# Where setup work and two convolution taps stand in the order of a fused convolution and feed-forward kernel

## The chip, the cores and the metric

The kernel runs on one core of one Trainium2 chip. The metric is the device time of one execution in microseconds (us); the time before the change is 2389.32 us, the median of three runs (2388.79 to 2389.75).

The core has a matrix engine (TensorE, PE in the profile), three engines for elementwise work (VectorE or DVE, ScalarE or ACT, GpSimd or POOL), and a queue (SyncE, SP) that issues the transfers used here. Each engine takes its instructions in the order in which the program gives them; engines wait for each other through semaphores.

## The reference

A depthwise causal convolution over seven tokens, whose taps come from a softmax and are shared within a head, is followed by a feed-forward block with the activation h * sigmoid(1.702 h). Everything is in 32-bit floats.

```python
# x: (8, 4096, 192), weight: (8, 7); w_in: (192, 2048), w_out: (2048, 192)
w = softmax(weight, axis=-1)
x_pad = concat([zeros((B, 6, D)), x], axis=1)
x_unf = x_pad[:, arange(S)[:, None] + arange(7)[None, :], :].reshape(B, S, 7, H, group)
a = einsum('hk,bskhg->bshg', w, x_unf).reshape(B * S, D)      # 32768 tokens x 192
h = a @ w_in
g = h * (1.0 / (1.0 + exp(-1.702 * h)))
out = g @ w_out
```

## The kernel before

The tokens are handled in 32 steps ("big" in the code) of 1024 tokens. A step has a part `hidden` (convolved tokens times w_in, then the activation) and a part `output` (times w_out). Both replace block products by fewer products of sums of blocks; T1 and T2 are such sums of activations, made by DVE. `hidden` runs twice per step, for `v` 0 and 1. What DVE has to prepare for a later step (turning x with three transposes, then 7 convolution taps for each of three groups of channels, then block sums) is kept in a list, `todo`. At fixed places the code calls `work(us)`, which hands DVE as many items from the list as the given time allows, by the cost noted with each item.

Before step 1 the weights are made ready. They arrive as 64-bit words and are turned into 32-bit floats in eight pieces, four of w_in (pieces 0 to 3) and four of w_out (4 to 7): a DVE part (`split_piece`), an ACT part (`split_rest`), then `join_piece` and `round_piece` on DVE. Step 0 is computed by plain products meanwhile (`plain`), since the sums of weights that the other steps use (`sums_w_in`) are not made yet. Blank lines are left out below.

```python
# load_x(big): eight transfers of x into xin, of which there is one buffer; xs below has its place too
# ... (cut)
# conv_t: 13 blocks of T columns per buffer, 3 buffers; TERMS lists the 21 products
at = [(osbs, 0), (flat_room, 3 * PIECE), (places, 0), (b22, 0)]
assert 5 * PIECE + R <= 10 * TOK and 2 * PIECE <= min((NA - 4 * NC) * UW, 4 * TOK)
raw = [t[:, i : i + 2 * PIECE].bitcast(U32) for t, i in at]
# ... (cut) scratch() cuts a place into three parts m, l, e
sets = [
    scratch(own(1).rearrange("p b t -> p (b t)")),
    scratch(flat_room),
    None,
    scratch(w_out_s[:, S1 : S4 + 1, :, :].rearrange("p i f d -> p (i f d)")),
]
SET = (0, 1, 2, 0, 1, 3, 1, 3)
# ... (cut)
def words(i):
    w = raw[i % NW].rearrange("p (n w) -> p n w", w=2)
    return (w[:, :, 0], w[:, :, 1]) + tuple(sets[SET[i]])
CLAMP = (0, 3, 4)
def split_piece(i):
    lo, hi, m, l, e = words(i)
    ef = e.bitcast(F32)
    vec.tensor_scalar(m, hi, 0xFFFFF, 1 << 20, op0=ALU.bitwise_and, op1=ALU.bitwise_or)
    vec.tensor_scalar(e, hi, 20, 0x7FF, op0=ALU.logical_shift_right, op1=ALU.bitwise_and)
    if i in CLAMP:
        vec.tensor_scalar(
            ef, e, float(LOW + 255), float(LOW), op0=ALU.min, op1=ALU.max
        )
def split_rest(i):
    lo, hi, m, l, e = words(i)
    ef = e.bitcast(F32)
    act.activation(l.bitcast(F32), lo, AF.Copy, scale=2.0**-32)
    if i in CLAMP:
        act.activation(e, ef, AF.Identity, bias=bias[:, 3:4], scale=2.0**23)
    else:
        act.activation(ef, e, AF.Relu, bias=bias[:, 0:1])
        act.activation(ef, ef, AF.Relu, bias=bias[:, 1:2], scale=-1.0)
        act.activation(e, ef, AF.Identity, bias=bias[:, 2:3], scale=-(2.0**23))
def join_piece(i):
    lo, hi, m, l, e = words(i)
    vec.tensor_tensor(out=m.bitcast(F32), in0=l.bitcast(F32), in1=m, op=ALU.add)
def round_piece(i, dsts):
    lo, hi, m, l, e = words(i)
    vec.scalar_tensor_tensor(
        out=e, in0=hi, scalar=1 << 31, in1=e, op0=ALU.bitwise_and, op1=ALU.bitwise_or
    )
    for view, dst in dsts:
        vec.scalar_tensor_tensor(
            out=dst,
            in0=view(m.bitcast(F32)),
            scalar=2.0**-20,
            in1=view(e.bitcast(F32)),
            op0=ALU.mult,
            op1=ALU.mult,
        )
# ... (cut) round_w_in(i): round_piece into w_in_s
def load_w_out(i):
    nc.sync.dma_start(
        out=raw[i].rearrange("p (c d) -> p c d", c=CW),
        in_=w_out_v[:, i * CW : (i + 1) * CW, :],
    )
def round_w_out(i):
    join_piece(NW + i)
    k, j = divmod(i * CW, NK)
    round_piece(
        NW + i,
        [
            (
                lambda v, m=m: v.rearrange("p (b m d) -> p b m d", m=2, d=Q)[:, :, m, :],
                w_out_s[:, 2 * m + k, j : j + CW, :].rearrange("p j (c d) -> p (j c) d", d=Q),
            )
            for m in range(2)
        ],
    )
# ... (cut)
def prepare(big):
    for c in range(NC):
        yield "", 0.7, lambda c=c: transpose_x(big, c)
    if big + 1 < N_BIG:
        yield "", 0.0, lambda: load_x(big + 1)
    v1 = place(big, V1)
    for c in (0, 2):
        for k in range(K):
            yield "", 0.76 if k else 0.48, lambda c=c, k=k: conv(big, c, k)
    yield "", 0.38, lambda: sums_c(big, 0)
    yield f"first {big}", 0.0, lambda: cross_when(True, big, v1, v1 + 1)
    for k in range(K):
        yield "", 0.76 if k else 0.48, lambda k=k: conv(big, 1, k)
    yield "", 0.0, lambda: cross_when(False, big, 0, C31)
    for i in range(1, len(SUMS_C)):
        yield "", 0.38, lambda i=i: sums_c(big, i)
    rest = (C31, V8) if big % 2 else (C31 + 1, NB)
    yield f"all {big}", 0.0, lambda: cross_when(False, big, *rest)
def product1(slot, a, b, big, v, first=False):
    pair = conv_t[:, big % 2 : big % 2 + 2, place(big, b), :]
    for h in range(2):
        src = pair[halves[h], :, :] if h == big % 2 else pair[halves[h], ::-1, :]
        nc.tensor.matmul(
            slot[:, h, :],
            w_in_s[halves[h], a, v * P : (v + 1) * P],
            src,
            start=first,
            stop=True,
            skip_group_check=True,
        )
def terms(big, v, slot, *ts, first=False):
    for t in ts:
        product1(slot, *TERMS[t], big, v, first)
        first = False
# ... (cut)
def sum_1(*a):
    sum_g(T1, B12, B11, *a)
def sum_2(*a):
    sum_g(T2, B22, T1, *a)
def plain(u, m, n, v, slot, ks=range(NC)):
    for k in ks:
        product1(slot, NC * (2 * u + m) + k, 2 * k + n, 0, v, k == ks[0])
def hidden(big, v, x, z, y, sums, work, fetch, last=lambda: None):
    def pe(slot, *ts, first=False):
        terms(big, v, slot, *ts, first=first)
    if v:
        pe(z, 7, first=True)
        give(True, big)
    pe(sums, 12)
    act.copy(k15, sums)
    pe(x, 5, 17)
    gelu(B11, 0, v, x)
    if not v:
        pe(z, 7, first=True)
    pe(sums, 0)
    act.copy(k16, sums)
    last()
    work(3.2 if v else 1.5)
    pe(y, 6, 14, first=True)
    vec.tensor_sub(x, z, k15)
    work(2.6)
    pe(sums, 13)
    act.copy(k19, sums)
    pe(x, 2)
    act.copy(k18, x)
    pe(z, 11)
    pe(sums, 20, 10)
    vec.tensor_sub(k15, y, k19)
    # ... (cut) more terms, copies and gelus, with work(1.1), work(2.3), work(1.2), work(0.7)
def output(big, ra, rb, work, cols=ALL, between=None, end=None):
    W = cols.stop - cols.start
    small = W < TOK
    js = slice(cols.start // Q, cols.stop // Q)
    v1, v2 = u1[:, 0:W], u2[:, 0:W]
    v3, v4 = p3[:, js, :], p4[:, js, :]
    some = dict(cols=cols, small=small)
    p1, p3c = product2(ra, 0, (A11, B11), (S4, B22, 0), **some)
    act.copy(v1, p1)
    act.copy(chunk(v3, 0), blocks(p3c))
    if not small:
        work(3.0)
        sum_1(0)
        sum_2(0)
    sum_1(1, cols, small)
    sum_2(1, cols, small)
    work(0.7)
    # ... (cut) the products p2, p6, p5 and p7, their additions, turns and stores, with work(0.7), work(4.0)
def work(us):
    while todo and todo[0][1] <= us + 0.2:
        us -= todo[0][1]
        todo.pop(0)[2]()
def need(label):
    while any(item[0] == label for item in todo):
        todo.pop(0)[2]()
# ... (cut)
def first_step(fetch):

    # ... (cut) the convolution of step 0, most of it on TensorE
    xs = xin_pool.tile([P, 2, NJ, XW], F32, name="xin")
    sets[2] = scratch(xs.rearrange("p n j d -> p (n j d)"))
    split_piece(0)
    split_rest(0)
    take_conv(2, 0)
    join_piece(0)
    round_w_in(0)
    load_w_out(0)
    split_piece(1)
    take_conv(1, 1)
    split_rest(1)
    for k in range(K):
        conv(0, 2, k, second)
    copy_over(C32)
    plain(0, 0, 0, 0, slots[0])
    plain(0, 0, 0, 1, sums)
    gelu(B11, 0, 0, slots[0])
    gelu(B11, 0, 1, sums)
    for k in range(K):
        conv(0, 0, k, second)
    copy_over(C12)
    plain(0, 0, 1, 0, slots[1], (1, 2, 0))
    plain(0, 0, 1, 1, slots[2])
    join_piece(1)
    round_w_in(1)
    load_w_out(1)
    split_piece(2)
    gelu(B12, 0, 0, slots[1])
    split_rest(2)
    gelu(B12, 0, 1, slots[2])
    def rounds(now, then):
        if now < NW:
            join_piece(now)
            round_w_in(now)
            load_w_out(now)
        else:
            round_w_out(now - NW)
        if then < 2 * NW:
            split_piece(then)
            split_rest(then)
    def last_piece():
        rounds(7, 8)
        sums_w_out()
        todo.extend(("", 0.42, lambda i=i: sums_w_in(i)) for i in range(len(SUMS_W)))
        todo.append(("sums", 0.0, lambda: None))
    def piece_3():
        rounds(3, 4)
        load_x(1)
        todo.extend(prepare(1))
    between = [
        lambda: rounds(2, 3), piece_3, None, lambda: rounds(4, 5), None, lambda: rounds(5, 6),
        None, lambda: rounds(6, 7), None, last_piece, None, None,
    ]
    free = [slots[0], sums, slots[1], slots[2]]
    for u, m in ((0, 1), (1, 0), (1, 1)):
        for n in range(2):
            for v in range(2):
                slot = free.pop(0)
                free.append(slot)
                plain(u, m, n, v, slot)
                gelu(2 * m + n, u, v, slot)
                (between.pop(0) or (lambda: work(1.3)))()
    give(False, 0)
    # ... (cut) step 0's first half of output by plain products, then need("all 1"),
    # prepare(2), output(0, ..., slice(T, TOK), fetch) and need("sums")
```

Of the kernel before, what the change touches and what calls it, by code (L numbers as in the profile page):

```python
# [15 lines left out]
def kernel(  # L16
# [38 lines left out]
    NC = D // R  # L55
# [150 lines left out]
    NW = 4  # L206
# [4 lines left out]
    places = w_in_s[:, 4 * NC : NA, :].rearrange("p a f -> p (a f)")  # L211
    b12, b22 = (g[:, b, 1, :, :, :].rearrange("p v h t -> p (v h t)") for b in (B12, B22))
    at = [(osbs, 0), (flat_room, 3 * PIECE), (places, 0), (b22, 0)]
    assert 5 * PIECE + R <= 10 * TOK and 2 * PIECE <= min((NA - 4 * NC) * UW, 4 * TOK)
    raw = [t[:, i : i + 2 * PIECE].bitcast(U32) for t, i in at]
    diag = b12[:, 0 : 2 * K * R].rearrange("p (c k q) -> p c k q", c=2, k=K)
# [55 lines left out]
        nc.gpsimd.memset(bias[:, i : i + 1], b)  # L272

    def words(i):
        w = raw[i % NW].rearrange("p (n w) -> p n w", w=2)
        return (w[:, :, 0], w[:, :, 1]) + tuple(sets[SET[i]])


# [65 lines left out]

    def load_w_out(i):
        nc.sync.dma_start(
            out=raw[i].rearrange("p (c d) -> p c d", c=CW),
            in_=w_out_v[:, i * CW : (i + 1) * CW, :],
        )

# [157 lines left out]
    def sum_1(*a):  # L508
        sum_g(T1, B12, B11, *a)
# [7 lines left out]
    def sum_4(*a):  # L517
        sum_g(T4, T2, B21, *a)

    def plain(u, m, n, v, slot, ks=range(NC)):  # L520

        for k in ks:
            product1(slot, NC * (2 * u + m) + k, 2 * k + n, 0, v, k == ks[0])

    def hidden(big, v, x, z, y, sums, work, fetch, last=lambda: None):

# [15 lines that stand above are left out]
        pe(sums, 0)  # L542
        act.copy(k16, sums)
        last()
        work(3.2 if v else 1.5)
        pe(y, 6, 14, first=True)
        vec.tensor_sub(x, z, k15)  # L547
        work(2.6)
# [7 lines that stand above are left out]
        gelu(B12, 0, v, sums)  # L556
        pe(x, 4)
        act.copy(k20, x)
        vec.tensor_sub(k19, z, k19)  # L559
        work(1.1)  # L560
        gelu(B22, 1, v, k19)
        gelu(B22, 0, v, k15)
        pe(y, 8)
        pe(sums, 1, 9, first=True)
        pe(y, 15)
        work(2.3)
        vec.tensor_add(k20, k20, sums)  # L567
        vec.tensor_sub(k16, y, k16)
        gelu(B11, 1, v, k20)
        pe(x, 18)  # L570
        gelu(B21, 1, v, x)
        fetch()
        if not v:

            act.copy(y, z)
        gelu(B21, 0, v, k16)
        work(1.2)
        pe(sums, 3, 19)
        work(0.7)
        vec.tensor_add(k18, k18, sums)  # L580
        return lambda: gelu(B12, 1, v, k18)
# [58 lines left out]
# [14 lines that stand above are left out]
            work(3.0)  # L654
            sum_1(0)
            sum_2(0)
        sum_1(1, cols, small)
        sum_2(1, cols, small)
        work(0.7)
        p2, p3c = product2(rb, 0, (A12, B21), (S4, B22, 1), **some)  # L660
        act.copy(chunk(v3, 1), blocks(p3c))  # L661
        vec.tensor_add(v2, v1, p2)
        turn(0, 0, blocks(v2), js)
        sum_4(0, cols, small)
        sum_4(1, cols, small)
        p6, p3c = product2(ra, 1, (S2, T2), (S4, B22, 2), **some)
        act.copy(chunk(v3, 2), blocks(p3c))
        vec.tensor_add(v2, v1, p6)
        sum_3(0, cols, False)
        sum_3(1, cols, False)  # L670
        work(0.7)
        if between:
            between()
        p5, p4c = product2(rb, 1, (S1, T1), (A22, T4, 0), **some)
        q = quarters(rb, 0, A22, T4, 2, **some)
        act.copy(chunk(v4, 0), blocks(p4c))  # L676
        vec.tensor_add(v1, v2, p5)  # L677
        act.copy(chunk(v4, 2), blocks(q[2]))
        vec.tensor_add(v3, blocks(v1), v3)  # L679
        for l in (0, 1, 3):  # L680
            vec.tensor_add(chunk(v4, 2), chunk(v4, 2), blocks(q[l]))  # L681
        turn(0, 1, v3, js)
        work(1.5 if small else 4.0)
        parts = [(cols, ra)]
        if end is not None:
            parts = [(slice(0, T), ra), (slice(T, TOK), end)]
        done = [product2(r, 0, (S3, T3), (A22, T4, 1), cols=c, small=small) for c, r in parts]
        for (c, _), (p7, p4c) in zip(parts, done):
            k = slice(c.start - cols.start, c.stop - cols.start)
            i = slice(c.start // Q, c.stop // Q)  # L690
            act.copy(chunk(p4, 1)[:, i, :], blocks(p4c))
            vec.tensor_add(v1[:, k], v1[:, k], p7)  # L692
            vec.tensor_add(v2[:, k], v2[:, k], p7)  # L693
            turn(1, 1, blocks(v1[:, k]), i)
            vec.tensor_sub(blocks(v2[:, k]), blocks(v2[:, k]), p4[:, i, :])  # L695
            turn(1, 0, blocks(v2[:, k]), i)
            store(big, i)
# [3 lines left out]
# [4 lines that stand above are left out]
# [27 lines left out]
    def first_step(fetch):  # L732
# [28 lines left out]
        for k in range(K):  # L761
            conv(0, 2, k, second)
        copy_over(C32)
        plain(0, 0, 0, 0, slots[0])
        plain(0, 0, 0, 1, sums)
        gelu(B11, 0, 0, slots[0])
# [1 line left out]
        for k in range(K):  # L768
            conv(0, 0, k, second)
        copy_over(C12)  # L770
        plain(0, 0, 1, 0, slots[1], (1, 2, 0))
        plain(0, 0, 1, 1, slots[2])
        join_piece(1)
        round_w_in(1)
        load_w_out(1)
        split_piece(2)
        gelu(B12, 0, 0, slots[1])
        split_rest(2)
        gelu(B12, 0, 1, slots[2])

        def rounds(now, then):
            if now < NW:
                join_piece(now)
                round_w_in(now)
                load_w_out(now)
            else:
                round_w_out(now - NW)
            if then < 2 * NW:
                split_piece(then)
                split_rest(then)  # L790

        def last_piece():
            rounds(7, 8)
            sums_w_out()
            todo.extend(("", 0.42, lambda i=i: sums_w_in(i)) for i in range(len(SUMS_W)))
            todo.append(("sums", 0.0, lambda: None))

        def piece_3():
            rounds(3, 4)
            load_x(1)  # L800
            todo.extend(prepare(1))

        between = [
            lambda: rounds(2, 3), piece_3, None, lambda: rounds(4, 5), None, lambda: rounds(5, 6),
            None, lambda: rounds(6, 7), None, last_piece, None, None,
        ]
        free = [slots[0], sums, slots[1], slots[2]]
        for u, m in ((0, 1), (1, 0), (1, 1)):
# [3 lines that stand above are left out]
                    free.append(slot)  # L812
                    plain(u, m, n, v, slot)
                    gelu(2 * m + n, u, v, slot)
                    (between.pop(0) or (lambda: work(1.3)))()
        give(False, 0)


# [4 lines left out]
            sum_1(u, slice(T, TOK), True)  # L823
            sum_2(u, slice(T, TOK), True)
        js = slice(0, T // Q)
        work(6.5)
        for k in range(2):
            for i, (m, n) in enumerate(quarter):
                c, c22c = product2(
                    slots[i % 2],  # L830
                    i // 2,
                    ((A11, A12, A21, A22)[2 * m + k], (B11, B12, B21, B22)[2 * k + n]),
                    ((A21, A22)[k], (B12, B22)[k], i),
                    first=(k == 0),
                    cols=cols,
                )
                if k == 1:
                    if i == 0:
                        vec.tensor_sub(*(w_out_s[:, j, :, :] for j in (S3, A11, A21)))
                    turn(m, n, blocks(c), js)  # L840
                    act.copy(chunk(c22, i), c22c)
                    work(2.5)
        turn(1, 1, blocks(c22), js)
        store(0, js)
        need("all 1")
# [59 lines left out]
```

## Time and profile before

| | busy us | share of the span (2387.3 us) | instructions |
|---|---|---|---|
| PE, matmuls | 2357.3 | 99% | 16794 |
| PEld, weight loads (beside the matmuls) | 889.5 | 37% | 16794 |
| DVE | 1946.2 | 82% | 2182 |
| ACT | 1023.3 | 43% | 1160 |
| POOL | 8.3 | 0% | 29 |

The transfers moved 133.66 MB, at a mean of 56 GB/s. Busy time counts an instruction from its start to its end as the trace has it; the ends of matmuls are modelled, and neighbours overlap a little. A group of instructions is written as line, engine, operation, tile written <- tiles read. "PE slot L486 <- DVE slot L547" in the list of waits means that a matmul of line 486 that writes the tile `slot` stood until DVE's instruction of line 547 on `slot` had ended. The lines that matter here: 286, 287 and 289 are `split_piece`; 297 to 304 `split_rest`; 308 `join_piece`; 313 and 317 `round_piece`; 332 to 340 sums of blocks (of weights in `w_in_s`, of tokens in `conv_t`); 346 loads a piece of w_out; 100 loads x; 408 turns x; 423 and 425 are convolution taps; 486 is `product1`, 503 the activation, 506 the sums such as T1 and T2, 547 the subtraction in `hidden` shown above, 590 a product of `output`, 625 a transpose of results.

### The profile page before, as it was taken

What the parts mean: (1) busy time and instruction counts of PE and PEld (TensorE: products, weight loads), DVE (VectorE), ACT (ScalarE), POOL (GpSimd) and SP (SyncE); (2) the same over time, 40 slices, a digit from 0 to 9 for tenths busy, and PEclk for the clock granted to TensorE, in tenths of its full rate; (3) what the DMA queues carried; (4) which work ended last, traced back from release to release, by engine and by line L of the source; (5) the groups of instructions that cost most, each with busy time, mean ns of one, the idle gap of its engine ahead of it and who ended that gap; (6) DMA issues with size and microseconds to landing.
All of it is one profiled execution on the core that took longest, in us unless ns stands there. A gap on an engine that the chain in (4) does not pass through costs nothing.

```text
span 2387.3 us, 39095 instructions
## 1 busy us (share of the span) xinstructions
PE 2357.3 (99%) x16794; PEld 889.5 (37%) x16794; DVE 1946.2 (82%) x2182; ACT 1023.3 (43%) x1160; POOL 8.3 (0%) x29
## 2 busy tenths in 40 slices
PE   8999999999999999999999999999999999999998
PEld 4533333333333333333333333333333333333333
DVE  6888887888887888878888778888788887788866
ACT  5345433454333554334543345543345433455433
POOL 1000000000000000000000000000000000000000
PEclk9999999999999999999999999999999999999999
DMA  7242133231232321323312323213233123231010
GB/s 164 59 79 55 28 65 61 59 67 32 52 65 54 68 54 29 65 58 62 67 30 54 65 55 68 52 32 64 58 64 68 27 56 66 54 67 43 16 41 14
DMA packets 197724, 133.66 MB, mean 56 GB/s; under 512 B 108848, under 2 KB 188080, under 8 KB 193584
## 3 DMA queue, kind: packets, MB, share of 16 engines
q1 hardware_dynamic: 196448, 130.92, 27.2%
q8 instruction: 131, 2.15, 0.4%
q10 hardware_dynamic: 1104, 0.26, 0.1%
q14 instruction: 41, 0.34, 0.0%
HBM read 53.15 MB, written 25.17 MB: 33 GB/s over the span
## 4 chain that ended last, share of the span: by engine, by line
PE 79%; DVE 17%; issue 1%; ACT 1%; DMA 1%; SPq 0%; ACTq 0%; DVEq 0%
PE slot L590 28%; PE slot L486 28%; PE sums L486 12%; PE sums L590 9%; DVE conv_t L425 5%; DVE osbs L681 3%; DVE osbs L625 3%; PE slot L607 2%; DVE slot L547 2%; DVE room L677 1%; DVE room L692 1%; DVE osbs L679 1%; DVE room L693 1%; ACT osbs L676 1%; DVE room L695 1%
## 5 line engine op out<-in xcount | busy, mean ns | idle before, releaser
L486 PE MATMUL slot<-conv_t,w_in_s 64*128 64x512 f32 x3740 | 863.3, 595 | 21.8 <-ACT g L503 8.5
L590 PE MATMUL slot<-g,w_out_s 128*32 128x512 f32 (+1 forms) x6800 | 788.6, 571 | 0.0
L486 PEld LDWEIGHTS slot<-conv_t,w_in_s 64*128 64x128 f32 x3740 | 358.1, 188 | 482.9 <-issue 381.2
L425 DVE SCALAR_TENSOR_TENSOR conv_t<-xt,cw,conv_t 128x512 f32<-128x512 f32 (+1 forms) x576 | 423.9, 736 | 11.9
L590 PEld LDWEIGHTS slot<-g,w_out_s 128*32 128x32 f32 x6800 | 240.3, 110 | 457.1 <-issue 438.3
L486 PE MATMUL sums<-conv_t,w_in_s 64*128 64x512 f32 x1660 | 405.1, 591 | 0.0
L503 ACT ACTIVATE g<-room 128x1024 f32<-128x1024 f32 x310 | 321.1, 1058 | 108.4 <-DVE room L567 68.6
L590 PE MATMUL sums<-g,w_out_s 128*32 128x512 f32 (+1 forms) x2304 | 335.0, 587 | 0.0
L506 DVE TENSOR_TENSOR g<-g 128x2048 f32<-128x2048 f32 (+1 forms) x126 | 283.1, 2267 | 4.7 <-PE slot L590 2.4
L486 PEld LDWEIGHTS sums<-conv_t,w_in_s 64*128 64x128 f32 x1660 | 158.5, 187 | 203.4 <-issue 159.6
L503 ACT ACTIVATE g<-slot 128x1024 f32<-128x1024 f32 x167 | 169.4, 1017 | 94.0 <-PE slot L486 94.0
L590 PEld LDWEIGHTS sums<-g,w_out_s 128*32 128x32 f32 x2304 | 93.1, 110 | 152.7 <-issue 146.3
L506 DVE TENSOR_TENSOR room<-g 128x2048 f32<-128x2048 f32 (+1 forms) x65 | 145.8, 2243 | 4.3
L506 DVE TENSOR_TENSOR g<-room,g 128x2048 f32<-128x2048 f32 (+1 forms) x64 | 140.2, 2229 | 0.0
L676 ACT COPY osbs<-slot 32x512 f32<-32x512 f32 (+1 forms) x32 | 18.3, 573 | 251.6 <-PE slot L607 251.6
L590 PE MATMUL slot<-room,w_out_s 128*32 128x512 f32 (+1 forms) x816 | 112.9, 567 | 0.0
L590 PE MATMUL sums<-room,w_out_s 128*32 128x512 f32 x768 | 112.7, 592 | 0.0
L677 DVE TENSOR_TENSOR room<-room,slot 96x512 f32<-96x512 f32 (+1 forms) x32 | 21.6, 675 | 91.2 <-ACT osbs L676 91.2
L661 ACT COPY osbs<-slot 32x512 f32<-32x512 f32 (+1 forms) x32 | 18.4, 573 | 175.6 <-PE slot L590 175.6
L547 DVE TENSOR_TENSOR slot<-slot,room 128x1024 f32<-128x1024 f32 x62 | 76.2, 1230 | 12.0 <-ACT g L503 10.2
L559 DVE TENSOR_TENSOR room<-slot,room 128x1024 f32<-128x1024 f32 x62 | 75.9, 1225 | 6.8 <-DVE room L555 0.5
L567 DVE TENSOR_TENSOR room<-room,sums 128x1024 f32<-128x1024 f32 x31 | 37.7, 1218 | 53.4 <-PE sums L486 53.4
(149 smaller groups left out, 1527.0 us busy)
## 6 DMA issues: line engine op xcount, KB each, us to landing
xin<-in_x_dram SPq DMA_DIRECT2D x240, 180.0 KB, 5.7
conv_t<-conv_t SPq DMA_DIRECT2D x62, 512.0 KB, 4.5
out_dram<-osbs SPq DMA_DIRECT2D x180, 128.0 KB, 2.5
conv_t<-conv_t SPq DMA_DIRECT2D x62, 256.0 KB, 3.6
conv_t<-conv_t SPq DMA_DIRECT2D x62, 64.0 KB, 1.9
xin<-in_x_dram SPq DMA_DIRECT2D x16, 160.0 KB, 5.2
out_dram<-osbs SPq DMA_DIRECT2D x20, 64.0 KB, 1.9
osbs<-in_moe_w_in_dram SPq DMA_DIRECT2D x2, 384.0 KB, 7.2
```

The costliest lines, as they stand in the source:

```text
L425: vec.scalar_tensor_tensor(out=dst, in0=src, scalar=tap, in1=dst, op0=ALU.mult, op1=ALU.add)
L486: nc.tensor.matmul(slot[:, h, :], w_in_s[halves[h], a, v * P : (v + 1) * P], src, start=first, stop=True, skip_group_check=True,)
L503: act.activation(g[:, b, u, v, :, :], src, AF.Gelu_apprx_sigmoid)
L506: vec.tensor_sub(*(half(x, u, cols, small) for x in (dst, a, b)))
L547: vec.tensor_sub(x, z, k15)
L559: vec.tensor_sub(k19, z, k19)
L590: nc.tensor.matmul(dst[l * Q : (l + 1) * Q, :], w_out_s[:, a, j, c * Q : (c + 1) * Q], half(b, u, cols, small)[:, v, h, :], start=(first a ...
L607: nc.tensor.matmul(dst[l], w_out_s[:, a, j, c * Q : (c + 1) * Q], half(b, u, cols, small)[:, v, h, :], start=(i == 0), stop=(i == NK // 4 ...
L625: vec.transpose(osb[:, n, js, m * Q : (m + 1) * Q], src)
L676: act.copy(chunk(v4, 0), blocks(p4c))
L677: vec.tensor_add(v1, v2, p5)
L681: vec.tensor_add(chunk(v4, 2), chunk(v4, 2), blocks(q[l]))
```

## The change

Four things are done.

1. In `hidden`, the place for prepared work ahead of the subtraction of line 547 is left out for `v` = 0. The work is not dropped: the list is handed out at the following places.
2. Setup splits each piece of the weights one piece further ahead of its rounding. Piece 2 is split before the first plain products, piece 3 before the stages, and so on. Piece 7 (the last of w_out) is loaded into `osbs` instead of a part of `g`, once piece 4 has left it, so its load and its rounding stand later.
3. x of step 1 is asked for right after piece 2 has been rounded, in stage 0 instead of stage 1, and the list that turns and convolves it (`prepare(1)`) is opened in stage 4. Until then DVE goes on with the weights.
4. `output` no longer makes T1 and T2 of `u` = 1 for the half step that ends step 0; `first_step` has made them already. The taps' places in setup are given other lengths, and the four last plain products of the first group are ordered so that those that need the last convolved block come last.

```diff
--- before.py
+++ after.py
@@ -211,6 +211,8 @@
     places = w_in_s[:, 4 * NC : NA, :].rearrange("p a f -> p (a f)")
     at = [(osbs, 0), (flat_room, 3 * PIECE), (places, 0), (b22, 0)]
+    at += at[0:3] + at[0:1]
     assert 5 * PIECE + R <= 10 * TOK and 2 * PIECE <= min((NA - 4 * NC) * UW, 4 * TOK)
     raw = [t[:, i : i + 2 * PIECE].bitcast(U32) for t, i in at]
     diag = b12[:, 0 : 2 * K * R].rearrange("p (c k q) -> p c k q", c=2, k=K)
@@ -272,7 +274,7 @@
         nc.gpsimd.memset(bias[:, i : i + 1], b)
     def words(i):
-        w = raw[i % NW].rearrange("p (n w) -> p n w", w=2)
+        w = raw[i].rearrange("p (n w) -> p n w", w=2)
         return (w[:, :, 0], w[:, :, 1]) + tuple(sets[SET[i]])
@@ -344,7 +346,7 @@
     def load_w_out(i):
         nc.sync.dma_start(
-            out=raw[i].rearrange("p (c d) -> p c d", c=CW),
+            out=raw[NW + i].rearrange("p (c d) -> p c d", c=CW),
             in_=w_out_v[:, i * CW : (i + 1) * CW, :],
         )
@@ -517,10 +519,10 @@
     def sum_4(*a):
         sum_g(T4, T2, B21, *a)
-    def plain(u, m, n, v, slot, ks=range(NC)):
+    def plain(u, m, n, v, slot, ks=range(NC), first=0):
         for k in ks:
-            product1(slot, NC * (2 * u + m) + k, 2 * k + n, 0, v, k == ks[0])
+            product1(slot, NC * (2 * u + m) + k, 2 * k + n, 0, v, k == first)
     def hidden(big, v, x, z, y, sums, work, fetch, last=lambda: None):
@@ -542,7 +544,8 @@
         pe(sums, 0)
         act.copy(k16, sums)
         last()
-        work(3.2 if v else 1.5)
+        if v:
+            work(3.2)
         pe(y, 6, 14, first=True)
         vec.tensor_sub(x, z, k15)
         work(2.6)
@@ -654,9 +657,9 @@
             work(3.0)
             sum_1(0)
             sum_2(0)
-        sum_1(1, cols, small)
-        sum_2(1, cols, small)
-        work(0.7)
+            sum_1(1)
+            sum_2(1)
+        work(4.5 if small else 0.7)
         p2, p3c = product2(rb, 0, (A12, B21), (S4, B22, 1), **some)
         act.copy(chunk(v3, 1), blocks(p3c))
         vec.tensor_add(v2, v1, p2)
@@ -761,6 +764,7 @@
         for k in range(K):
             conv(0, 2, k, second)
         copy_over(C32)
+        split_piece(2)
         plain(0, 0, 0, 0, slots[0])
         plain(0, 0, 0, 1, sums)
         gelu(B11, 0, 0, slots[0])
@@ -768,41 +772,53 @@
         for k in range(K):
             conv(0, 0, k, second)
         copy_over(C12)
-        plain(0, 0, 1, 0, slots[1], (1, 2, 0))
-        plain(0, 0, 1, 1, slots[2])
+        split_rest(2)
+        for ks in (1, 2), (0,):
+            plain(0, 0, 1, 0, slots[1], ks, 1)
+            plain(0, 0, 1, 1, slots[2], ks, 1)
         join_piece(1)
         round_w_in(1)
         load_w_out(1)
-        split_piece(2)
         gelu(B12, 0, 0, slots[1])
-        split_rest(2)
         gelu(B12, 0, 1, slots[2])
-        def rounds(now, then):
-            if now < NW:
-                join_piece(now)
-                round_w_in(now)
-                load_w_out(now)
-            else:
-                round_w_out(now - NW)
-            if then < 2 * NW:
-                split_piece(then)
-                split_rest(then)
-        def last_piece():
-            rounds(7, 8)
+        def split(i):
+            split_piece(i)
+            split_rest(i)
+        def rounds(i):
+            join_piece(i)
+            round_w_in(i)
+        def stage_0():
+            rounds(2)
+            load_w_out(2)
+            load_x(1)
+            split(4)
+        def stage_1():
+            rounds(3)
+            split(5)
+        def stage_2():
+            round_w_out(0)
+            load_w_out(3)
+            split(6)
+        def stage_4():
+            round_w_out(1)
+            todo.extend(prepare(1))
+        def last_stage():
+            round_w_out(3)
             sums_w_out()
             todo.extend(("", 0.42, lambda i=i: sums_w_in(i)) for i in range(len(SUMS_W)))
             todo.append(("sums", 0.0, lambda: None))
-        def piece_3():
-            rounds(3, 4)
-            load_x(1)
-            todo.extend(prepare(1))
-        between = [
-            lambda: rounds(2, 3), piece_3, None, lambda: rounds(4, 5), None, lambda: rounds(5, 6),
-            None, lambda: rounds(6, 7), None, last_piece, None, None,
+        split(3)
+        stages = [
+            stage_0, stage_1, stage_2, None, stage_4, None, None, lambda: split(7),
+            None, lambda: round_w_out(2), None, last_stage,
         ]
         free = [slots[0], sums, slots[1], slots[2]]
         for u, m in ((0, 1), (1, 0), (1, 1)):
@@ -812,7 +828,7 @@
                     free.append(slot)
                     plain(u, m, n, v, slot)
                     gelu(2 * m + n, u, v, slot)
-                    (between.pop(0) or (lambda: work(1.3)))()
+                    (stages.pop(0) or (lambda: work(2.3)))()
         give(False, 0)
@@ -823,7 +839,7 @@
             sum_1(u, slice(T, TOK), True)
             sum_2(u, slice(T, TOK), True)
         js = slice(0, T // Q)
-        work(6.5)
+        work(5.0)
         for k in range(2):
             for i, (m, n) in enumerate(quarter):
                 c, c22c = product2(
@@ -839,7 +855,7 @@
                         vec.tensor_sub(*(w_out_s[:, j, :, :] for j in (S3, A11, A21)))
                     turn(m, n, blocks(c), js)
                     act.copy(chunk(c22, i), c22c)
-                    work(2.5)
+                    work(2.8)
         turn(1, 1, blocks(c22), js)
         store(0, js)
         need("all 1")
```

## What the change should do to the time, predicted blind

> **What bounds the kernel now.** The busy table says that TensorE (PE) works 2357.3 of 2387.3 us, so time can only come from the 30 us in which it stands, or from stretches in which it runs slowly. The list of PE's waits says where it stands:
>
> ```profile
> PE slot L486 <- ACT g L503: 8.5, 1, 8.5
> PE slot L486 <- DVE slot L547: 8.5, 28, 0.3
> PE slot L486 <- DVE w_in_s L332: 3.7, 1, 3.7
> PE slot L486 <- DVE room L308: 1.0, 1, 1.0
> ```
>
> (us in total, times, longest.) Three of the four are single events of the setup; the second comes once in almost every step. To place them I took busy times by stretch (length, then PE, PEld, DVE, ACT, POOL busy with instruction counts, granted PE clock, DMA share, GB/s):
>
> ```profile
> 18.40:27.40 9.00, 8.02 (x40) 3.50 (x38) 8.55 (x17) 7.53 (x11) 0.00 (x0) 1.00 0.75 185
> 27.40:50.90 23.50, 23.45 (x110) 10.27 (x106) 11.08 (x16) 13.50 (x15) 0.00 (x0) 1.00 0.68 164
> 50.90:59.40 8.50, 0.00 (x0) 0.00 (x0) 7.45 (x12) 3.76 (x5) 0.00 (x0) 0.72 0.26 59
> 59.40:72.60 13.20, 13.20 (x48) 5.54 (x48) 10.24 (x18) 12.28 (x14) 0.00 (x0) 0.79 0.44 75
> 72.60:112.80 40.20, 40.20 (x726) 23.46 (x724) 37.16 (x58) 5.59 (x12) 0.00 (x0) 1.00 0.24 55
> 112.80:117.60 4.80, 1.14 (x8) 0.30 (x4) 4.70 (x15) 1.38 (x2) 0.00 (x0) 0.85 0.20 43
> 117.60:122.90 5.30, 5.27 (x12) 2.19 (x14) 3.99 (x9) 1.02 (x1) 0.00 (x0) 0.50 0.16 35
> ```
>
> PE does nothing from 50.9 to 59.4, and the granted clock sinks to 0.72 and 0.79; it stands again before 117.6 and then runs at 0.50. Matmul starts are 0.2145 us apart at full clock (12 of line 486 in 2.57 us); the 12 from 117.63 take some 5.3 us. So each long wait is paid for twice.
>
> Who is behind the wait for ACT? DVE's timeline, with the releaser of its idle time in brackets:
>
> ```profile
> 39.93 0.56 DVE L289 TENSOR_SCALAR room<-room 128x768 f32<-128x768 uint32 x1
> 50.39 1.44 DVE L408 STREAM_TRANSPOSE xt<-xin 128x576 f32<-128x576 f32 x2 [9.90 <-DMA xin<-in_x_dram]
> 54.52 0.55 DVE L286 TENSOR_SCALAR w_out_s<-room 128x768 uint32<-128x768 uint32 x1
> ```
>
> The transposes of x of step 1 stand in DVE's order ahead of the weights, and x lands only at 49.98. DVE idles 9.9 us; so the split of piece 5 (line 286, 54.52) is late, ACT's rest of it (line 302, 55.57) too, the activation queued behind that starts at 58.44, and PE waits for it.
>
> In a steady step (73.1 us), DVE's timeline around the first subtraction of line 547 reads:
>
> ```profile
> 780.18 0.71 DVE L625 STREAM_TRANSPOSE osbs<-room 96x512 f32<-96x512 f32 x1
> 780.82 1.49 DVE L425 SCALAR_TENSOR_TENSOR conv_t<-xt,cw,conv_t 128x512 f32<-128x512 f32 x2
> 782.23 1.23 DVE L547 TENSOR_TENSOR slot<-slot,room 128x1024 f32<-128x1024 f32 x1
> ```
>
> and PE's:
>
> ```profile
> 782.18 1.02 PE L486 MATMUL slot<-conv_t,w_in_s 64*128 64x512 f32 x4
> 783.51 4.56 PE L486 MATMUL slot<-conv_t,w_in_s 64*128 64x512 f32 x20 [0.30 <-DVE slot L547]
> ```
>
> Two taps stand right ahead of the subtraction, and PE waits 0.30 us for it.
>
> **What the skill says.** The Trainium skill, page "TensorE: Matmul & The Clock Gate", section Part 1, gives 215.7 ns between warm matmuls of 512 columns, half the rate when cold, and a fall to cold after an idle window of about 3.4 us. The trace agrees: 214.5 ns, clock 0.50 after 3.69 us of idling, and no fall after the 0.98 us ahead of 26.55. The same page ("Engine queue depths") says that ACT and DVE are strict FIFO: hence the blocked chain above. "VectorE: DVE Perf Modes", the section on mode 2x_2P, says that an fp32 tensor_tensor stays at the 1x rate; at the page's 0.96 GHz, 1024 elements are 1.07 us by estimate, and the trace has 1.22 (line 506). So no DVE work gets cheaper here; it can only be left out or moved.
>
> **The steady steps.** `work(1.5)` gave two taps (1.49 us). Without it line 547 starts when the turn is done, at 780.89 instead of 782.23, and ends at about 782.1. The matmul that needs it is free at 782.18 + 4 x 0.2145 = 783.04, so the wait goes, with 0.9 us to spare. ACT's copy of line 543, which the turn of line 625 also holds, ends at 781.99 and its matmul starts at 782.18 without a gap; the change doesn't touch it. Where do the taps go? The list shifts by two: the later places of `v` = 0 stay as full as before, and the end of the list moves into `v` = 1. There `work(3.2)` now holds four taps (3.0 us, against two taps and four sums in 3.1), and the seven sums, 7 x 0.36 = 2.5 us, follow line 547, pushing line 555 from 802.89 to about 803.2 while PE needs its result after 805.6. DVE then idles 3.34 us (before line 567), so it has room. Gain: 28 x 0.30 = **8.5 us**, the whole row.
>
> **The setup, part by part.** Durations from the page before: split on DVE 1.0 us (1.5 with the clamp), join and rounding 2.9, rest on ACT 3.7 (1.9 with the clamp), activation 0.95, a plain product of 12 matmuls 2.57, a quarter product 64 x 0.0545 = 3.5.
>
> - First products. The 1.0 us split of piece 2 now stands ahead of the taps of the last convolved block, so that block reaches `conv_t` at 27.45 instead of 26.5. PE has 16 matmuls of the reordered group first (23.7 to 27.15), then the last 8: ready at 29.4, against 30.0 before, with 0.5 us idle. Piece 1 is rounded at 29.4, so stage 0 begins then.
> - x. Rounding of piece 2 ends near 33.8 and x is asked for at 34.2, against 38.4. From the first issue to the last landing it took 49.98 - 38.41 = 11.6 us, so it lands near 45.8. DVE meanwhile does pieces 3, 4 and 5: split 4 to 35.3, rounding 3 to 38.2, split 5 to 39.2, rounding 4 to 42.05, split 6 to 43.0, rounding 5 to 46.0. The transposes then find x there. The 9.9 us wait goes.
> - ACT. Its order is now dense: rest of 3 to 34.9, an activation, rest of 4 to 37.7, an activation, rest of 5 to 42.4, activation 2 to 43.3, rest of 6 to 47.1, activations 3 and 4. Stage 7 uses the tile of stage 3, whose activation ends at 48.0, while PE is ready at 47.6: 0.5 us. After that ACT is ahead.
> - PE ends stage 11 at 29.4 + 12 x 2.57 + 0.5 + small starts = **61**, against 72.6: 11.6 us. Of this 8.5 is the wait, 0.6 the reordering and about 2.5 the slow clock.
> - Piece 7 is asked for at 42.05 behind x and lands near 50; its split at 50.1, its rest by 55.5, its rounding from 58.4 to 61.3. The k = 1 products need it after 61 + 3 x 3.5 = 71.5. No wait.
> - From 61 the 40.2 us of the stretch 72.6 to 112.8 follow unchanged: end near 101.2. DVE is done with the sums of w_out at 64.2, with T1 and T2 at 69.1, six taps at 73.7; the turns follow PE; "all 1" by 85. Leaving out two sums of line 506 saves 2 x 1.22 = 2.45 us; `work(4.5)` then takes 11 sums of weights, the later places 2 and 4. Three of 20 are left at the end, against 12 before, which is what PE waited 3.69 us for. They end near 105, and step 1 asks for the last one near 107. So this wait goes with its slow clock: 3.69 + 2.7 = 6.4 us.
>
> Sum for the setup: 11.6 + 6.4 = **18 us**; with the steps 26.5 us, or 2362.8. I add about one microsecond for waits I have not seen: **2364 us**, 1.1% less.
>
> **The rivals.** *DVE takes DMA's place.* DVE is 37.16 us busy in the 40.2 from 72.6; if the tail of the list isn't ready at 107, PE waits again. For it: my margin is only 2 us. Against it: 9.9 us of idling and 2.45 us of sums are gone ahead of it. If it held, some 3.7 us and the slow clock would stay: about 2370. *ACT becomes the bound in the stages.* ACT has no idle time from 27.5 to 51.7 in my plan, and every microsecond that it slips shows at stage 7. It would cost 1 to 3 us, or 2365 to 2367; if x or piece 7 lands 3 us late the same holds, since DVE has slack until 75. *The moved taps come back as another wait* (line 555 or 567): then the 8.5 us shrink or stay, about 2368 to 2372. Against it are the 3.34 us that DVE idles in `v` = 1. *All fits:* 2389.3 - 8.5 - (8.5 + 3.7 + 1.0 + some 5.3 of slow clock) = 2362.3 is near the floor.
>
> **Range and chances.** The floor gives the low end, 2360, with 2 us for what I round. The high end, 2371, is one of the rivals in full. A gain over 2% would need 48 us, more than PE's whole idle time; a loss of 2% would need a new wait of 1.5 us in every step. Faster by over 2%: 0.01; within 2%: 0.98; slower: 0.01.
>
> **What would show it.** Right: the row for line 547 is gone from PE's waits; DVE's row for xin is near zero; stage 11 ends near 61; no PE wait near 100 to 118; the granted clock is 1.00 from 27 on. Wrong: a new row of 0.2 us or more some 30 times (steps), or a wait of over 2 us between 27 and 110 with the clock falling after it (setup).

## The result, and the profile after

The changed kernel takes 2354.16 us (2353.64 to 2354.82) against 2389.06 us in the same session: ratio 0.9854, interval 0.9837 to 0.9871. It is 34.9 us faster. The prediction had 2364 with a range from 2360 to 2371, so the gain is 10 us larger than foreseen.

In the changed file the lines have moved by two or three: 486 is 488, 503 is 505, 547 is 550, 408 is 410, 425 is 427, 590 is 593, 607 is 610. The busy row of TensorE (PE) after, and the whole list of PE's waits after:

```profile
PE 2343.5 (100%) x16794; PEld 890.8 (38%) x16794; DVE 1951.4 (83%) x2180; ACT 1019.4 (43%) x1160; POOL 8.3 (0%) x29
```

```profile
PE sums L389 <- POOL osbs masks.py:199: 1.4, 1, 1.4
PE slot L400 <- POOL bias L274: 0.5, 1, 0.5
```

All four waits are gone. What is left lies in the first 5 us, ahead of any product, and was there before. Busy times by stretch of the setup, in the columns of the prediction's table:

```profile
18.40:27.40 9.00, 9.00 (x48) 3.79 (x40) 8.57 (x19) 7.55 (x12) 0.00 (x0) 1.00 0.77 187
27.40:61.00 33.60, 33.60 (x166) 14.96 (x168) 32.79 (x49) 30.02 (x34) 0.00 (x0) 1.00 0.75 159
61.00:101.00 40.00, 40.00 (x722) 23.38 (x712) 34.50 (x61) 5.11 (x12) 0.00 (x0) 1.00 0.24 55
101.00:110.00 9.00, 9.00 (x44) 4.07 (x42) 8.10 (x15) 5.05 (x6) 0.00 (x0) 1.00 0.34 79
```

PE is busy without a gap and the clock stays at 1.00. DVE is busy for 32.79 of the 33.6 us of the stages. It no longer idles for x, which was issued at 33.57 and had landed by 45.24:

```profile
44.34 1.03 DVE L319 SCALAR_TENSOR_TENSOR w_out_s<-w_out_s 128x384 f32<-128x384 f32 x2
45.62 2.10 DVE L410 STREAM_TRANSPOSE xt<-xin 128x576 f32<-128x576 f32 x3 [0.25 <-issue]
```

In a steady step the subtraction follows the transpose at once, and the three taps come after it:

```profile
756.63 0.71 DVE L628 STREAM_TRANSPOSE osbs<-room 96x512 f32<-96x512 f32 x1
757.27 1.20 DVE L550 TENSOR_TENSOR slot<-slot,room 128x1024 f32<-128x1024 f32 x1
758.38 2.30 DVE L427 SCALAR_TENSOR_TENSOR conv_t<-xt,cw,conv_t 128x512 f32<-128x512 f32 x3
```

and PE runs through it (24 matmuls where before there were 4, a gap and 20):

```profile
756.91 1.88 PE L488 MATMUL sums<-conv_t,w_in_s 64*128 64x512 f32 x8
758.63 5.32 PE L488 MATMUL slot<-conv_t,w_in_s 64*128 64x512 f32 x24
763.78 1.02 PE L488 MATMUL sums<-conv_t,w_in_s 64*128 64x512 f32 x4
```

**Where the time came from.** One group of matmuls (line 607, now 610) occurs once per step, so the distance of its starts is the period of a step, with nothing modelled in it:

| | before | after | gained |
|---|---|---|---|
| start in step 0 | 108.38 | 96.14 | 12.24 |
| from step 0 to step 1 | 74.76 | 68.17 | 6.59 |
| period of a steady step | 73.01 | 72.44 | 0.57 |
| from step 1 to step 30 | 2117.46 | 2100.72 | 16.74 |
| from step 30 to the end | 86.7 | 86.7 | 0.0 |

(The rows add up to 35.6 us, the difference of the two profiled executions; the medians differ by 34.9.) The setup gave 18.8 us, where 18 was predicted. The steps gave 16.7, where 8.5 was predicted: a step became 0.57 us shorter, though the row of waits had shown 0.30.

The theory that I tested (A): the row is only a part of what a wait costs. The prediction's own numbers say so. The four matmuls at 782.18 leave PE free at 783.04, and the next starts at 783.51, 0.47 us late. The row shows 0.30 because the last matmul's modelled end is 783.20 (782.18 + 1.02). After the gap the 20 matmuls take 783.51 to 787.90, 4.39 us instead of 20 x 0.2145 = 4.29: 0.10 more. 0.47 + 0.10 = 0.57. Rivals: the rest of the 0.57 came from the transfers and the start, which other parts of the change moved (B), or from the new order of the taps at the other places in a step (C).

### The profile page after: what moved, and what is told of

The parts are those of the page before. It is cut to its first block, busy times and chain, and to the rows that moved or that the text cites. A ratio compares the mean times of both kernels' runs of the same rounds, so it can differ in the third digit from the quotient of the medians.

```text
span 2351.7 us, 39068 instructions
## 1 busy us (share of the span) xinstructions
PE 2343.5 (100%) x16794; PEld 890.8 (38%) x16794; DVE 1951.4 (83%) x2180; ACT 1019.4 (43%) x1160; POOL 8.3 (0%) x29
## 4 chain that ended last, share of the span: by engine, by line
PE 99%; DVE 0%; POOL 0%; ACT 0%; issue 0%; ACTq 0%; POOLq 0%
PE slot L488 34%; PE slot L593 33%; PE sums L488 15%; PE sums L593 14%; PE slot L610 2%; PE slot L723 0%; DVE osbs L628 0%; DVE osbs L684 0%; POOL osbs L261 0%; PE sums L389 0%; PE slot L400 0%; PE slot L389 0%; DVE room L695 0%; DVE room L680 0%; DVE osbs L682 0%
## 5 line engine op out<-in xcount | busy, mean ns | idle before, releaser
L488 PE MATMUL slot<-conv_t,w_in_s 64*128 64x512 f32 x3740 | 852.0, 590 | 0.0
```

The source lines that it names most:

```text
L488: nc.tensor.matmul(slot[:, h, :], w_in_s[halves[h], a, v * P : (v + 1) * P], src, start=first, stop=True, skip_group_check=True,)
```

## The experiments

"Before" and "changed" name the kernel that was edited. The reference of each comparison was measured anew, at 2389.5 to 2389.7 us.

**e1: the moved taps alone, in the kernel before.**

```diff
-        work(3.2 if v else 1.5)
+        if v:
+            work(3.2)
```

> The kernel before with part 1 alone: no prepared work ahead of line 547 for v = 0. Theory A (each wait costs a step 0.57 us, from one matmul's start to the next, and the 0.30 us in the list of waits is only the part after the modelled end of the last matmul): the period of the steps falls from 73.01 to 72.44 us, the time by 29 x 0.57 = 16.5 us to 2372.5. Theory B (the row of waits gives the whole cost, 0.30; the other 0.27 us of each step came with the earlier start or other timing of the transfers that parts 2 to 4 bring): the period falls to 72.71, the time to 2380.6.

Measured: 2372.16 us (ratio 0.993, 0.9918 to 0.9942); period 72.44. In PE's waits the setup's two long rows stay and the row for line 547 is gone:

```profile
PE slot L486 <- ACT g L503: 8.7, 1, 8.7
PE slot L486 <- DVE w_in_s L332: 3.7, 1, 3.7
```

So B is out: part 1 alone gives 17.3 us.

**e2: the same place put back, in the changed kernel.**

```diff
-        if v:
-            work(3.2)
+        work(3.2 if v else 1.5)
```

> The changed kernel with work(1.5) put back for v = 0. Theory A: period 73.01 us, time 2354.2 + 16.5 = 2370.7. Theory B: period 72.74, time 2354.2 + 8.5 = 2362.7.

Measured: 2371.10 us (0.9924, 0.9911 to 0.9936); period 73.01. The row is back as it was:

```profile
PE slot L488 <- DVE slot L549: 8.5, 28, 0.3
```

8.5 us in the row are 16.9 us of time.

**e3, e9, e10: other work at the same place.** In the changed kernel n subtractions whose result nobody reads are put ahead of line 547; the order of the taps is that of the change. n is 2 in e3, 1 in e9, 3 in e10.

```diff
         if v:
             work(3.2)
+        else:
+            for _ in range(n):
+                vec.tensor_sub(spare, w_in_s[NC * Q : P, 0:2, :], w_in_s[NC * Q : P, 2:4, :])
```

> The changed kernel with two added DVE subtractions (32 partitions x 512 elements, result not used) ahead of line 547 for v = 0, so that the order of the taps stays as changed and only that line is late, by about 2 x 0.68 = 1.36 us against 1.49 for the two taps. Theory A (the wait itself costs more than its row says): the row for line 547 in PE's waits shows about 0.25 to 0.30 us each and the period rises by 0.5 to 0.57 us, to about 73.0; time near 2354.2 + 31 x 0.55 = 2371. Theory C (the 0.27 us beyond the row came from the new order of the taps at the other places of a step): the period rises by the row alone, to 72.7; time near 2363.

> The changed kernel with one added DVE subtraction ahead of line 547 for v = 0 (0.68 us). With two of them PE started 0.61 us after it was free and the period rose by 0.71 us (row of waits 0.45). One of them moves the end of the subtraction 0.7 us forward, to about 0.1 us before PE is free. Theory A (loss = lateness of the matmul's start over the time at which PE was free, plus 0.10 us of restart, and nothing if it isn't late): no row for line 555, period 72.44 us, time 2354.2. Rival (work ahead of the subtraction costs in proportion): period near 72.8, time 2365.

> The changed kernel with three added DVE subtractions there. Theory A: the matmul starts 0.70 us later than with two, so the row shows 0.45 + 0.70 = 1.15 us each, and the period rises by that and the same fixed 0.26 us: 72.44 + 1.41 = 73.85 us; time near 2375.7 + 30 x 0.70 = 2396.7. Rival (the part beyond the row grows with the row, at the ratio 0.71 / 0.45): period 72.44 + 1.8 = 74.25, time 2409.

PE's timeline of e3 in one step (the subtraction is line 555 there):

```profile
764.79 1.02 PE L488 MATMUL slot<-conv_t,w_in_s 64*128 64x512 f32 x4
766.26 4.56 PE L488 MATMUL slot<-conv_t,w_in_s 64*128 64x512 f32 x20 [0.45 <-DVE slot L555]
770.65 1.02 PE L488 MATMUL sums<-conv_t,w_in_s 64*128 64x512 f32 x4
```

and of e10:

```profile
771.25 1.02 PE L488 MATMUL slot<-conv_t,w_in_s 64*128 64x512 f32 x4
773.44 1.99 PE L488 MATMUL slot<-conv_t,w_in_s 64*128 64x512 f32 x8 [1.16 <-DVE slot L555]
```

| added operations | row, us each | time, us | period | period over 72.44 | less the row |
|---|---|---|---|---|---|
| 0 (the change) | none | 2354.16 | 72.44 | 0 | |
| 1 (e9) | none | 2354.80 | 72.44 | 0 | |
| two taps (e2) | 0.30 | 2371.10 | 73.01 | 0.57 | 0.27 |
| 2 (e3) | 0.45 | 2375.65 | 73.15 | 0.71 | 0.26 |
| 3 (e10) | 1.16 | 2396.99 | 73.87 | 1.43 | 0.27 |

Theory A holds at every dose. Work that keeps the subtraction ahead of PE costs nothing; once PE waits, the loss is the row plus a fixed 0.26 to 0.27 us, not a multiple of the row. C is out, since in e3, e9 and e10 the taps' order was the changed one throughout. The added time is also found whole at this one place: in e3 the next matmul starts 0.61 us after PE is free (764.79 + 4 x 0.2145 = 765.65) and the 20 matmuls take 4.39 us, 0.10 too long, together 0.71. In e3 I had expected the subtraction's end some 0.15 us too early, hence 2375.65 and not 2371; the row was longer by the same amount.

**e4: the end of setup alone, in the kernel before.**

```diff
             sum_2(0)
-        sum_1(1, cols, small)
-        sum_2(1, cols, small)
-        work(0.7)
+            sum_1(1)
+            sum_2(1)
+        work(4.5 if small else 0.7)
```

> The kernel before with the end of setup alone changed: T1 and T2 of u = 1 made once, and work(4.5) instead of work(0.7) at that place. My theory: DVE gains 2.45 us of sums and the 2.0 us that it idles ahead of line 677, enough for the nine further sums of weights (9 x 0.38 = 3.4 us), so PE's wait of 3.69 us before step 1 goes and with it the slow clock after it (about 2.7 us): time 2389.1 - 6.4 = 2382.7. Rival (a wait costs its own length only): 2389.1 - 3.7 = 2385.4.

Measured: 2383.09 us (0.9974, 0.9965 to 0.9984), a gain of 6.4. The wait for `w_in_s` has left the list, and the 12 matmuls behind it take 2.57 us to the next start, where the prediction's table has 5.3 us at a clock of 0.50:

```profile
113.81 2.74 PE L486 MATMUL slot<-conv_t,w_in_s 64*128 64x512 f32 x12
116.38 1.02 PE L486 MATMUL sums<-conv_t,w_in_s 64*128 64x512 f32 x4
```

That is the 3.7 of the row and 2.7 of slow clock.

**e5: the two sums left out, and nothing put in their place.**

```diff
-        sum_1(1, cols, small)
-        sum_2(1, cols, small)
+            sum_1(1)
+            sum_2(1)
         work(0.7)
```

> The kernel before with T1 and T2 of u = 1 made once and the place after them left at work(0.7). My theory: DVE is 2.45 us earlier, but meets the wait ahead of line 677, which PE's products set: that wait grows from 2.0 to about 4.5 us, the same twelve sums of weights are left at the end, and the time stays at 2389.1 (within 0.5). Rival (work that is taken off DVE shortens the setup by its length): 2386.6, or 2384 with the slow clock.

Measured: 2390.22 us (1.0002, 0.9994 to 1.001): no gain. DVE's waits of e5:

```profile
DVE room L677 <- ACT osbs L676: 2.0, 1, 2.0
DVE room L662 <- ACT osbs L661: 1.9, 1, 1.9
```

Of the 2.45 us, 1.9 went into a wait, but not into the one that I had named: DVE now idles 1.9 us at line 662, where it didn't in setup before, and line 677 stays at 2.0. Less DVE work alone was worth nothing; with `work(4.5)` in its place (e4) it was worth 6.4. Whether `work(4.5)` would have been enough with the two sums kept was not run.

**e6: x "asked for" later, in the changed kernel.**

```diff
             load_w_out(2)        # stage_0
-            load_x(1)
             split(4)
             rounds(3)            # stage_1
+            load_x(1)
             split(5)
```

> The changed kernel with x of step 1 asked for in stage 1, after piece 3, about 4 us later than in the change, and turned in stage 4 as in the change. My theory: x lands near 50 and DVE waits some 4 us for it, but PE still has products ahead and DVE catches up at the three turns of results for which it waits on PE now (0.83 + 0.80 + 0.54 us) and at line 680 (2.2 us): time 2354.2 to 2355.5, so that turning later is what pays and asking sooner hardly matters. Rival: the wait goes through to PE, 2358 or more.

Measured: 2354.39 us, and no wait for x at all. The experiment did not do what I had written. The queue that issues transfers goes through its own instructions; none of them stands between the two places in the text, so x was issued at 34.32 (33.57 in the change), not 4 us later. Even these 0.75 us are not the edit's: in this execution the transfer before, the load of piece 5, already went out 0.71 us later (28.98, against 28.27). The time says nothing about late x; e11 does.

**e7: x turned early, in the changed kernel.** The list for step 1 is opened in stage 2, with `work(2.3)` (three transposes) ahead of the rounding of piece 4.

```diff
         def stage_2():
+            todo.extend(prepare(1))
+            work(2.3)
             round_w_out(0)
         def stage_4():
             round_w_out(1)
-            todo.extend(prepare(1))
```

> The changed kernel with x asked for as early as in the change, but the list for step 1 opened, and the three transposes put, in stage 2 ahead of the rounding of piece 4. My theory: DVE waits about 7 us for x with the weights behind it, ACT's rest of piece 6 and the activation of stage 3 slip to about 55, PE waits 8 to 9 us at stage 7 and runs slowly after it: 2354.2 + 11 = 2365. Rival (DVE has the slack): 2354 to 2357.

Measured: 2364.22 us (0.9893, 0.9878 to 0.9909), 10.1 more than the change. The chain of the kernel before is back. DVE, and PE below it:

```profile
45.13 2.10 DVE L410 STREAM_TRANSPOSE xt<-xin 128x576 f32<-128x576 f32 x3 [6.33 <-DMA xin<-in_x_dram]
```

```profile
54.93 7.84 PE L488 MATMUL slot<-conv_t,w_in_s 64*128 64x512 f32 x24 [7.04 <-ACT g L505]
62.61 2.74 PE L488 MATMUL sums<-conv_t,w_in_s 64*128 64x512 f32 x12
```

DVE stands 6.3 us for x, ACT behind it, PE 7.0 us; then 24 matmuls take 7.7 us to the next start instead of 24 x 0.2145 = 5.1 (the granted clock was 0.67 from 54.9 to 62.4). Asked for as soon as in the change (33.64), x still costs 10 us if it is turned before it is there.

**e8: part 3 alone, in the kernel before.**

```diff
             rounds(2, 3)         # stage 0
+            load_x(1)
             rounds(3, 4)         # stage 1
-            load_x(1)
-            todo.extend(prepare(1))
             rounds(5, 6)         # stage 5
+            todo.extend(prepare(1))
```

> The kernel before with part 3 alone: x asked for in stage 0, the list for step 1 opened in stage 5 after piece 5 is rounded, splits as before. My theory: the 9.9 us wait of DVE and PE's 8.5 us wait go, with 2 to 2.5 us of slow clock; the waits of DVE for ACT at each rounding (1.0 to 1.8 us) stay, and the 3.7 us wait before step 1 stays as it is: 2389.1 - 10.5 = 2378.6. If the splitting one ahead was needed too, PE still waits some us in the stages: 2381 or more.

Measured: 2379.01 us (0.9955, 0.9942 to 0.9967), a gain of 10.5. PE's waits of e8:

```profile
PE slot L486 <- DVE slot L547: 8.5, 28, 0.3
PE slot L486 <- DVE w_in_s L332: 3.7, 1, 3.7
PE slot L486 <- DVE room L308: 1.4, 1, 1.4
```

The wait for ACT is gone, and DVE's waits for ACT at the roundings, which stay (0.8 to 2.1 us), don't reach PE in the stages. Part 3 makes two moves, x asked for sooner (here at 34.42) and turned later; e7 takes back the second one in the changed kernel, e11 the first.

**e11: x behind the load of piece 7, in the changed kernel.**

```diff
             load_w_out(2)        # stage_0
-            load_x(1)
             split(4)
             load_w_out(3)        # stage_2
+            load_x(1)
             split(6)
```

> The changed kernel with the transfers of x put behind the load of piece 7 in the order of the queue that issues transfers. That load waits until piece 4 is rounded (40.5), so x is issued near 41 and lands 11 us later, near 52, while its transposes are still put after piece 5 (45.6). My theory: DVE waits 6 to 7 us for x; 4.4 us of this are absorbed where DVE waits for PE now, the rest reaches PE late, in the products of step 0's output: 2358 to 2360. Rivals: all is absorbed (2354.2), or the whole wait comes through with a slow clock (2363).

Measured: 2360.07 us (0.9876, 0.9862 to 0.9889), 5.9 more than the change. x is issued from 41.14 on, right behind that load (40.72). DVE:

```profile
53.53 2.10 DVE L410 STREAM_TRANSPOSE xt<-xin 128x576 f32<-128x576 f32 x3 [7.91 <-DMA xin<-in_x_dram]
```

PE's waits:

```profile
PE slot L593 <- ACT room L857: 2.5, 1, 2.5
PE slot L593 <- ACT g L505: 1.7, 1, 1.7
...
PE slot L488 <- DVE room L310: 0.6, 1, 0.6
```

Of 7.9 us, 4.2 reach PE in the products of step 0 (the row of 0.6 belongs to the first products; this execution took 2358.72 us). So a place in the queue that issues x 7.6 us later costs 5.9 us here. In the kernel before, x also stood behind the load of piece 7, which was issued at 37.99, once piece 3 was rounded, and x at 38.41. Part 2 moves that load behind x even where the text asks for x late (e6); in e8 part 3 alone has the same effect, since it moves x. What those 4.8 us (38.41 against 33.57) cost in the kernel before was not measured by themselves.

**e12: three parts at once, in the kernel before.** The edits of e1, e4 and e8; pieces are split as before and the first products keep their order.

```diff
-        work(3.2 if v else 1.5)
+        if v:
+            work(3.2)
-        work(0.7)                # with sum_1(1), sum_2(1) as in e4
+        work(4.5 if small else 0.7)
             rounds(2, 3)         # prepare(1) after rounds(5, 6) as in e8
+            load_x(1)
```

> The kernel before with three edits at once: no taps ahead of line 547 for v = 0; x asked for in stage 0 and its list opened in stage 5; T1 and T2 once with work(4.5). Pieces are split as before, none further ahead. If the gains are independent they add up: 17.3 + 6.4 + 10.5 = 34.2 us, or 2355.2, so that splitting further ahead is worth 1 us. Rival (only the splitting ahead frees DVE enough for the sums of weights to be ready at the end of setup): a wait for w_in_s of 1 us or more is left before step 1, and the time is 2357 or more.

Measured: 2356.11 us (0.986, 0.9845 to 0.9875). No wait for `w_in_s` is left; the period is 72.44. The longest wait of PE past the first 5 us is one at the first products, where the changed kernel's trace has none (those of e2, e6 and e11, whose first products are the same, have 0.4 to 0.7 us):

```profile
PE slot L486 <- DVE room L308: 1.4, 1, 1.4
```

The parts add up to within 1 us. Everything else in the diff (splitting further ahead, the reordered first products, piece 7's other place, the other lengths of the taps' places) is left with 1.9 us of the 34.9 in all. No version beats the change.

## Why the prediction was wrong, step by step

**The steady steps: mechanism right, size wrong.** The step that failed reads: "Gain: 28 x 0.30 = 8.5 us, the whole row." The term is 0.57 per step, 29 steps, 16.7 us. I had read how long a wait was off the list, although I had just written that the matmul was free at 783.04 and shown that it started at 783.51. Of the 10 us by which the forecast missed, 8.2 are this term, 0.8 the setup and about 1 the allowance for waits that did not come. The taps found room in `v` = 1 as said, line 558 (555 before) isn't late, and no new wait came (e1, e2).

**The floor was built on the same row.** "2362.3 is near the floor" took all waits off the list and put 2360 under them. With 16.7 for 8.5 the same sum gives 2354.1. A floor worked out from rows that understate a wait isn't one. For the same reason it was wrong that time could only come from the 30 us in which PE stands or from slow stretches: PE's busy time itself fell from 2357.3 to 2343.5 us with 16794 matmuls both times, and 29 x 0.27 = 7.8 of these 13.8 us are what the steps' waits cost beyond their row.

**The setup: right.** Predicted 11.6 + 6.4, measured 12.24 + 6.59. Here I had worked from start to start through a plan, not from rows. Stage 11 ended at 60.39 (61), the products of step 0 at 100.57 (101.2), x was there at 45.24 (45.8). The two small waits of 0.5 us that I had planned, at the first products and at stage 7, are not in this trace; the one at the first products comes in some executions (0.65 us in e2, 0.44 in e6).

**x: right, with half of the reason.** I let x be asked for when piece 2 is rounded, and so it was: the rounding that frees its place ended at 33.50, and x was issued at 33.57. What I did not say is that nothing blocked may stand ahead of it in its queue: with the load of piece 7 there it went out at 41.14 (e11).

**The sums: right.** "So this wait goes with its slow clock: 3.69 + 2.7 = 6.4 us"; e4 measured 6.4. But leaving out T1 and T2 did not bring it alone (e5); it took `work(4.5)` as well (e4).

**The rivals.** DVE as the new bound at the end of setup and ACT in the stages did not come about. The chain through ACT is there and costs 10 us when DVE turns x too early (e7). A late DVE costs 6 us (e11), but in the products of step 0 and not, as I had feared, at the last sums of weights. A new wait for the moved taps did not appear.

## What to carry to other kernels

Take what a wait costs from the starts on both sides of it, or from the period of the loop, and not from the row of idle time: here a short wait in every turn cost 0.57 us, almost twice its row of 0.30. Ask of each piece of filler work what stands right behind it: work whose result nobody needs was free here only as long as the operation behind it still ended before PE needed that one (e9, e3). And look at what stands ahead of a transfer in its queue: one that waits holds up the rest (e11).

## What the runs showed that I had not expected

A wait of PE between matmuls of 512 columns (fp32, 64 rows, two halves side by side) costs its row plus 0.26 to 0.27 us, at rows of 0.30, 0.45 and 1.16: 0.16 because the last matmul's modelled end lies after the time at which the next could have started, and 0.10 in the first two matmuls after it. Both can be read from single starts: these matmuls start in pairs, the two halves 0.007 us apart and the pairs 0.43 us apart (0.2145 is the mean), while each is modelled as 0.59 us long; after a wait the second pair follows 0.53 us behind the first, in the kernel before, in e3 and in e10 alike. Why it takes 0.10 longer is not shown. Waits of 1.16 us in each step did not bring the clock down (its mean in e10 was 1.00); after those of 3.69 us (before) and 7.04 us (e7) it was 0.50 and 0.67.
